# Orders of a slot's steps by table, and two groups of casts on ScalarE: bucketed attention and a gated convolution on one core

## Chip, core and metric

The kernel runs on one core of a Trainium2 chip. The metric is the device time of one execution in microseconds (us). Engines are named as in the profile: PE (TensorE matmuls), PEld (its weight loads), DVE (VectorE), ACT (ScalarE), POOL (GpSimd), and SP, whose queue issues nearly all DMAs.

## The reference, cut to what matters

```python
# attention: B, H, S, D = 4, 8, 768, 64; proj is 64 x 6
q_bits = einsum(q, proj) > 0;  k_bits = einsum(k, proj) > 0       # 6 sign bits: a bucket
mask = q_bucket[..., :, None] == k_bucket[..., None, :]
scores = where(mask, q @ k.T / sqrt(D), -1e9)
attn = exp(scores - max);  attn = attn / (sum(attn) + 1e-9)
x = (attn @ v), heads side by side                               # (4, 768, 512)
# then, per batch
gate = sigmoid(causal convolution of x over the sequence, 5 taps, per channel)
out = (gate * (x @ w_val)) @ w_out                               # 512 x 512 each
```

## The kernel before, in words

There are 32 units (batch, head), each with six tiles of 128 queries: 192 tiles. The main loop runs over slots k = 0 to 195, and slot k works on several tiles at once:

- K, `keep_transposed(k-4)`: two ACT copies (L325) move the transposed probabilities out of PSUM into `pt`. After the sixth tile of a unit it queues `attn_v` for that unit.
- M, F, H, `maxima`, `factors`, `shifts` of tile k: the row maximum and two small DVE steps (L276, L282, L286). R and I, `row_sums` and `recip`, are the DVE's reciprocals for a pair of tiles (L298, L302), in even slots.
- Z, `normalise(k-2)`: POOL multiplies the probabilities by the reciprocals (L307).
- S, `scores(k+1)`: four matmuls (L270) into one of the **two** score buffers `s`. It can start only when the exponential of tile k-1 has read that buffer.
- E, `exponentials(k)`: ACT's exponential with its row sum (L292).
- T, `transposes(k-3)`: six PE transposes (L316) into the two PSUM buffers `tp`, freed by the next slot's K.
- A, one step of `attn_v`: two matmuls (L339; four in the trace, which counts the two parts of each); six steps make a unit, and the last one adds two ACT copies `x` (L347).
- C, one step of `pair_x`, after each second head: first two casts `xh` to fp32r (L359) with their remainders `xl` on POOL (L360), then five convolution steps on DVE (L368, L370), and after the fourth pair of a batch the sigmoids.
- G, one step of `moe`: four matmuls of `x @ w_val` (L401) or of the product with `w_out` (L425). After a value row block the DVE writes the gated values `ht` (L406); in the next G they are cast to `hh` (L410) and POOL makes the remainder `hl` (L412).
- P, one step of `prep` for the next unit: POOL's cast `aq` (L191), POOL's remainder `bq` (L194), six DMAs on SP (L195 to L198, L208, L209), and once in four units the sign bits: twice four matmuls (L226; eight in the trace) into a `tp` buffer and a DVE step `u` (L229).
- W, one step of the weights' decoding: eight parts of 512 columns with five DVE steps, one DVE cast (L113) and two POOL steps (L115, L118) each.

Every slot has the order K M R F I Z H S E C W G P A A T, with A A in odd slots alone, C in odd slots alone up to k = 59, and 1, 0, 2, 0, 2, 2 steps W by k mod 6. PE, ACT, DVE and POOL take their instructions in exactly the order in which this loop writes them; each engine works its own queue in order. SP's order is left to the framework. In the texts below a *head* is the six slots of one unit; the *early stage* is the slots up to 59, with no G yet; the *filled stage* is slots 60 to 191. About a quarter of the filled stage's slots have no G left, since a batch's steps run out before the next batch's sigmoids.

Of the kernel before, what the change touches and what calls it, by code (L numbers as in the profile page):

```python
# [20 lines left out]
TINY = float(2.0 ** -126)  # L21

LEAST = float(2.0 ** -15)


@with_exitstack
def kernel(
# [57 lines left out]
    wo = [const.tile([P, NP, 512], FP32R, name=f"wo{i}") for i in range(2)]  # L85

    def magnitudes(w, t):
        nc.scalar.activation(out=t, in_=w[:, :, 1].bitcast(FP32), func=AF.Abs)  # L90
        return t
# [17 lines left out]
    def split_weight(w, m, hi, lo, ahead):  # L109
        if w.dtype == I32:  # L110
            a, d = yield from from_float64(w, m, ps_m.tile([P, 512], FP32, name="m"))
            yield
            nc.vector.tensor_copy(out=hi, in_=a)  # L113
            yield
            nc.gpsimd.tensor_tensor(out=a, in0=a, in1=hi.bitcast(FP32), op=ALU.subtract)  # L115
            ahead()
            yield
            nc.gpsimd.tensor_tensor(out=lo, in0=a, in1=d, op=ALU.add)  # L118
        else:
            nc.vector.tensor_copy(out=hi, in_=w)  # L120
            ahead()
            yield
            nc.gpsimd.tensor_tensor(out=lo, in0=w, in1=hi.bitcast(FP32), op=ALU.subtract)
# [149 lines left out]
    def maxima(k):  # L273
        s = ss[k]
        nm = small.tile([P, 1], FP32, name="nm")
        nc.vector.tensor_reduce(out=nm, in_=s[:, :, 0:HS], axis=AX.XY, op=ALU.max, negate=True)  # L276
        nms[k] = nm

    def factors(k):

        gs[k] = small.tile([P, 1], FP32, name="gs")
        nc.vector.tensor_scalar(out=gs[k], in0=nms[k], scalar1=BIG / 2, scalar2=scale, op0=ALU.is_lt, op1=ALU.mult)  # L282
# [36 lines left out]
    def keep_transposed(k):  # L319
        i, qt = tiles[k]  # L320
        if qt % 3 == 0:
            cur["pts"].append([ptp.tile([P, 3, HS], FP32, name="pt") for _ in range(2)])
        qo = (qt % 3) * P
        for pt, tp in zip(cur["pts"][-1], tps.pop(k)):
            nc.scalar.copy(out=pt[:, :, qo:qo + P], in_=tp[:, 0:HS].rearrange("p (a b) -> p a b", b=P))  # L325
        if qt == KB - 1:
            avs.append(attn_v(i, cur["pts"]))
            cur["pts"] = []
# [24 lines left out]
    def pair_x(b, c, x, gs, xs_):  # L353
        for o in (0, HS):
            xh = xs.tile([P, HS], FP32R, name="xh")
            xl = xs.tile([P, HS], FP32R, name="xl")
            xs_[(c, o)] = (xh, xl)
            x0 = x[:, KW - 1 + o:KW - 1 + o + HS]
            nc.vector.tensor_copy(out=xh, in_=x0)  # L359
            nc.gpsimd.tensor_tensor(out=xl, in0=x0, in1=xh.bitcast(FP32), op=ALU.subtract)  # L360
        yield
        g = gp.tile([P, S], FP32, name="g")
        gs.append(g)
        for k in range(KW):
            yield
            w = cw_sb[:, c * KW + k:c * KW + k + 1]
            if k == 0:
                nc.vector.tensor_scalar(out=g, in0=x[:, 0:S], scalar1=w, scalar2=None, op0=ALU.mult)  # L368
            else:
                nc.vector.scalar_tensor_tensor(out=g, in0=x[:, k:k + S], scalar=w, in1=g, op0=ALU.mult, op1=ALU.add)  # L370
        if c == NP - 1:
            yield
# [13 lines left out]
    def moe(b, xs_, g):  # L386
        hs = {}
        todo = []

        def later():  # L390
            while todo:
                todo.pop(0)()

        def val(o, j):
            acc = acc_tile()
            m = 0
            for wi, xi in ((0, 0), (1, 0), (0, 1)):
                if m:
                    yield
                for c in range(NP):  # L400
                    nc.tensor.matmul(out=acc[:, 0:HS], lhsT=wv[wi][:, c, j * P:(j + 1) * P],  # L401
                                     rhs=xs_[(c, o)][xi], start=(m == 0), stop=(m == 11))
                    m += 1
                later()
            ht = hp.tile([P, HS], FP32, name="ht", bufs=2)
            nc.vector.tensor_tensor(out=ht, in0=acc[:, 0:HS], in1=g[j][:, o:o + HS], op=ALU.mult)  # L406

            def split():
                hh = hp.tile([P, HS], FP32R, name="hh")
                nc.vector.tensor_copy(out=hh, in_=ht)  # L410
                hl = hp.tile([P, HS], FP32R, name="hl")
                nc.gpsimd.tensor_tensor(out=hl, in0=ht, in1=hh.bitcast(FP32), op=ALU.subtract)  # L412
                hs[(o, j)] = (hh, hl)
            todo.append(split)
            yield

        def outp(o, tb):
            finish(weights)
            acc = acc_tile()
            m = 0  # L420
            for hi, wi in ((0, 0), (0, 1), (1, 0)):
                if m:
                    yield
                for j in range(NP):
                    nc.tensor.matmul(out=acc, lhsT=hs[(o, j)][hi][:, tb * P:(tb + 1) * P],  # L425
                                     rhs=wo[wi][:, j, :], start=(m == 0), stop=(m == 11))
                    m += 1
                later()
            ob = op.tile([P, 512], FP32, name="o")
            if cur["gates"]:  # L430
                nc.vector.tensor_copy(out=ob, in_=acc)
            else:
                nc.scalar.copy(out=ob, in_=acc)
            r0 = o + tb * P
            nc.sync.dma_start(out=out[b, r0:r0 + P, :], in_=ob)
            yield

        def idle(n):
            for _ in range(n):
                later()  # L440
                yield

        def hold():
            while len(moes) < 2 and not cur["end"]:
                yield
# [31 lines left out]
    with tc.manual_schedule(engines=ENGINES):  # L477
        for i in range(5):
            load_raw(i)
        load_values(0)  # L480
        first_prep()
        weights = [load_conv(), load_weights()]
        first_signs()
        preps = [prep(1)]
        step(preps)
        scores(0)
        load_raw(5)
        for gen in weights:
            next(gen)
        for k in range(N + LAG + 1):  # L490
            if 0 <= k - LAG - 1:
                keep_transposed(k - LAG - 1)
            pair = k % 2 == 0 and 0 <= k - 2 < N
            if k < N:
                maxima(k)
            if pair:
                row_sums(k - 2)
            if k < N:
                factors(k)
            if pair:  # L500
                recip(k - 2)
            if 0 <= k - 2 < N:
                normalise(k - 2)
            if k < N:
                shifts(k)
            if k + 1 < N:
                if tiles[k + 1][0] != tiles[k][0]:
                    finish(preps)
                    preps = [prep(tiles[k + 1][0] + 1)]
                scores(k + 1)  # L510
            if k < N:
                exponentials(k)
            if k >= 60 or k % 2:
                step(convs)
            for _ in range((1, 0, 2, 0, 2, 2)[k % 6] if k >= 8 else 0):
                step(weights)
            for _ in range(3 if cur["gates"] else 1):
                step(moes)
            cur["gates"] = max(0, cur["gates"] - 1)
            step(preps)  # L520
            if k % 2:
                step(avs)
                step(avs)
            if 0 <= k - LAG < N:
                transposes(k - LAG)
# [67 lines left out]
```

## Time and profile before

| what | us |
|---|---|
| median of 3 runs | 624.64 (624.13 to 624.96) |
| the profiled execution's own time | 624.6 |
| its span (first to last instruction) | 622.8 |
| slot 0's maximum starts | 10.7 |
| the last tile's maximum starts | 562.1 |

The profile's page gives busy time of each engine over the span. The table of stretches gives the same for a stretch of time. A timeline row has start, duration, engine, line, operation, tiles, count of merged instructions, and, in brackets, how long the engine was idle before it and whose end released it. The span lies 1.8 us under the execution's time, before and after the first and last instruction.

### The profile page before, as it was taken

What the parts mean: (1) busy time and instruction counts of PE and PEld (TensorE: products, weight loads), DVE (VectorE), ACT (ScalarE), POOL (GpSimd) and SP (SyncE); (2) the same over time, 40 slices, a digit from 0 to 9 for tenths busy, and PEclk for the clock granted to TensorE, in tenths of its full rate; (3) what the DMA queues carried; (4) which work ended last, traced back from release to release, by engine and by line L of the source; (5) the groups of instructions that cost most, each with busy time, mean ns of one, the idle gap of its engine ahead of it and who ended that gap; (6) DMA issues with size and microseconds to landing.
All of it is one profiled execution on the core that took longest, in us unless ns stands there. A gap on an engine that the chain in (4) does not pass through costs nothing.

```text
span 622.8 us, 10649 instructions
## 1 busy us (share of the span) xinstructions
PE 587.7 (94%) x3496; PEld 422.6 (68%) x3496; DVE 437.3 (70%) x1032; ACT 420.6 (68%) x881; POOL 376.3 (60%) x362
## 2 busy tenths in 40 slices
PE   5889889889999999999999999999999999999997
PEld 2755555556667777776667776677667777775885
DVE  5687999998757756686757867478675877565632
ACT  3787887777787676577786766677787766765300
POOL 4656878677747665486646766458654776453221
PEclk9799999999999999999999999999999999999999
DMA  8533437333422344233324333233422224100111
GB/s 270 144 99 88 125 109 198 95 102 91 130 51 82 80 123 115 48 88 99 107 80 114 82 98 84 86 82 82 122 55 77 68 47 107 46 19 1 51 52 51
DMA packets 23270, 56.77 MB, mean 91 GB/s; under 512 B 4296, under 2 KB 4296, under 8 KB 23216
## 3 DMA queue, kind: packets, MB, share of 16 engines
q1 hardware_dynamic: 23072, 56.06, 33.4%
q8 instruction: 28, 0.46, 0.3%
q14 instruction: 26, 0.21, 0.1%
q10 hardware_dynamic: 144, 0.03, 0.0%
HBM read 23.12 MB, written 6.29 MB: 47 GB/s over the span
## 4 chain that ended last, share of the span: by engine, by line
PE 69%; ACT 16%; DVE 9%; issue 2%; DMA 1%; POOL 1%; SPq 0%; ACTq 0%; DVEq 0%; POOLq 0%
PE av L339 19%; PE s L270 16%; PE tp L316 13%; PE m L425 8%; ACT p L292 7%; PE m L401 7%; ACT pt L325 5%; DVE nm L276 3%; ACT x L347 3%; PE tp L226 2%; PE tp L425 1%; PE s L425 1%; PE s L401 1%; PE tp L401 1%; DVE g L370 1%
## 5 line engine op out<-in xcount | busy, mean ns | idle before, releaser
L307 POOL TENSOR_SCALAR p<-p,ri 128x768 f32<-128x768 f32 x192 | 208.4, 1090 | 166.1 <-DVE nb L286 142.4
L276 DVE TENSOR_REDUCE nm<-s 128x1 f32<-128x768 f32 x192 | 182.5, 951 | 63.3 <-PE s L270 63.0
L325 ACT COPY pt<-tp 128x384 f32<-128x384 f32 x384 | 166.4, 485 | 87.9 <-PE tp L316 86.8
L292 ACT ACTIVATE p<-s,nb,gs 128x768 f32<-128x768 f32 x192 | 192.6, 1003 | 37.6 <-DVE nb L286 36.4
L316 PEld LDWEIGHTS tp<-ident,p 128*128 128x128 f32 x1152 | 129.8, 141 | 75.9 <-issue 48.1
L316 PE MATMUL tp<-ident,p 128*128 128x128 f32 x1152 | 165.9, 280 | 5.9 <-DVE u L229 2.3
L339 PE MATMUL av<-pt,vt 128*64 128x384 f32 x768 | 144.9, 499 | 0.0
L270 PE MATMUL s<-ak,aq 76*128 76x384 f32 x384 | 116.6, 385 | 20.0 <-ACT p L292 19.2
L270 PE MATMUL s<-bk,bq 128*128 128x384 f32 x384 | 100.0, 341 | 0.0
L339 PEld LDWEIGHTS av<-pt,vt 128*64 128x64 f32 x768 | 47.0, 136 | 62.7 <-issue 62.0
L270 PEld LDWEIGHTS s<-ak,aq 76*128 76x128 f32 x384 | 58.5, 192 | 33.6 <-ACT p L292 32.6
L370 DVE SCALAR_TENSOR_TENSOR g<-x,cw_sb,g 128x768 f32<-128x768 f32 x64 | 78.4, 1226 | 0.2
L270 PEld LDWEIGHTS s<-bk,bq 128*128 128x128 f32 x384 | 70.6, 191 | 0.0
L412 POOL TENSOR_TENSOR hl<-ht,hh 128x384 fp32r<-128x384 f32 x32 | 32.2, 1005 | 47.9 <-DVE hh L410 47.9
L194 POOL TENSOR_TENSOR bq<-r,aq 128x768 fp32r<-128x768 f32 x31 | 57.0, 1840 | 0.1
L347 ACT COPY x<-av 64x384 f32<-64x384 f32 x64 | 30.3, 473 | 31.9 <-PE av L339 31.4
L401 PE MATMUL m<-xh,wv 128*128 128x384 f32 x200 | 43.0, 339 | 0.0
L286 DVE TENSOR_SCALAR nb<-nm,gs 128x1 f32<-128x1 f32 x192 | 39.9, 208 | 3.5
L360 POOL TENSOR_TENSOR xl<-x,xh 128x384 fp32r<-128x384 f32 x32 | 33.4, 1060 | 14.2 <-DVE xh L359 14.2
L406 DVE TENSOR_TENSOR ht<-m,g 128x384 f32<-128x384 f32 x25 | 13.9, 555 | 37.5 <-PE m L401 32.9
L292 ACT ACTIVATION_READ_ACCUMULATOR p<-s,nb,gs 128x1 f32 x192 | 39.2, 204 | 0.0
L425 PE MATMUL m<-wo,hh 128*128 128x512 f32 x144 | 38.4, 396 | 0.0
(88 smaller groups left out, 475.0 us busy)
## 6 DMA issues: line engine op xcount, KB each, us to landing
r<-in_qk_dram SPq DMA_DIRECT2D x32, 384.0 KB
vt<-in_v_dram SPq DMA_DIRECT2D x16, 384.0 KB
out_dram<-o SPq DMA_DIRECT2D x24, 256.0 KB
ak<-aq SPq DMA_DIRECT2D x31, 192.0 KB
bk<-aq SPq DMA_DIRECT2D x31, 192.0 KB
bk<-bq SPq DMA_DIRECT2D x31, 192.0 KB
bq<-aq SPq DMA_DIRECT2D x31, 192.0 KB
w<-in_w_val_dram SPq DMA_DIRECT2D x4, 512.0 KB
```

Of the source, the lines that this page charges most:

```text
L194: nc.gpsimd.tensor_tensor(out=bq, in0=r, in1=aq.bitcast(FP32), op=ALU.subtract)
L270: nc.tensor.matmul(out=s[:, hf, 0:HS], lhsT=lq[0:n, qs], rhs=rk[0:n, hf * HS:(hf + 1) * HS], start=n == M, stop=n == P)
L276: nc.vector.tensor_reduce(out=nm, in_=s[:, :, 0:HS], axis=AX.XY, op=ALU.max, negate=True)
L292: nc.scalar.activation(out=p, in_=s[:, :, 0:HS], func=AF.Exp, bias=nb, scale=gs.pop(k), accum_out=sm[:, k % 2, 0:1])
L307: nc.gpsimd.tensor_scalar(out=p, in0=p, scalar1=rcs.pop(k), scalar2=1.0, op0=ALU.mult, op1=ALU.mult)
L316: nc.tensor.transpose(out=tp[:, n * P:(n + 1) * P], in_=p[:, kb * P:(kb + 1) * P], identity=ident)
L325: nc.scalar.copy(out=pt[:, :, qo:qo + P], in_=tp[:, 0:HS].rearrange("p (a b) -> p a b", b=P))
L339: nc.tensor.matmul(out=av[s * D:(s + 1) * D, 0:HS], lhsT=vt[:, kb, hh * D:(hh + 1) * D], rhs=pt[kb // 3][:, kb % 3, :], start=(kb == 0), s ...
L347: nc.scalar.copy(out=x[hh * D:(hh + 1) * D, o:o + HS], in_=av[s * D:(s + 1) * D, 0:HS])
L370: nc.vector.scalar_tensor_tensor(out=g, in0=x[:, k:k + S], scalar=w, in1=g, op0=ALU.mult, op1=ALU.add)
L401: nc.tensor.matmul(out=acc[:, 0:HS], lhsT=wv[wi][:, c, j * P:(j + 1) * P], rhs=xs_[(c, o)][xi], start=(m == 0), stop=(m == 11))
L425: nc.tensor.matmul(out=acc, lhsT=hs[(o, j)][hi][:, tb * P:(tb + 1) * P], rhs=wo[wi][:, j, :], start=(m == 0), stop=(m == 11))
```

## The change

Three things are changed. (1) The order of a slot's steps comes from a table: six strings for k < 60, by k mod 6, and twelve for k from 60 on, by k mod 12. A letter stands for one step as listed above. (2) The casts `xh` and `hh` are ACT copies; they were DVE copies. (3) In the weights' decoding, the fetched next part's magnitudes (an ACT step, `ahead`) come after the part's last POOL step and not before it; W runs from k = 7 on, six steps per six slots, and from k = 60 on 25 per twelve.

```diff
+START = 60
+EARLY = ["MKRFIHWCCWZPSECT", "MRSKFGGGIHZECPT", "MKGARSFIZHWECPT",
...
+LATE = ["MKRSFIHWZEGWWPCT", "MRKFSWWIHPZPCGWEAPAWT", "MKRSFHIZEGCGWWWT",
...
             nc.gpsimd.tensor_tensor(out=a, in0=a, in1=hi.bitcast(FP32), op=ALU.subtract)
+            yield
+            nc.gpsimd.tensor_tensor(out=lo, in0=a, in1=d, op=ALU.add)
             ahead()
-            yield
-            nc.gpsimd.tensor_tensor(out=lo, in0=a, in1=d, op=ALU.add)
...
-            nc.vector.tensor_copy(out=xh, in_=x0)
+            nc.scalar.copy(out=xh, in_=x0)
...
-                nc.vector.tensor_copy(out=hh, in_=ht)
+                nc.scalar.copy(out=hh, in_=ht)
...
-        for gen in weights:
-            next(gen)
+        next(weights[0])
+        next(weights[1])
         for k in range(N + LAG + 1):
...
+            o = EARLY[k % 6] if k < START else LATE[k % 12]
+            for act in o:
+                if act == "K" and 0 <= k - LAG - 1:
+                    keep_transposed(k - LAG - 1)
...
+                elif act == "C" and (k >= 60 or k % 2):
+                    step(convs)
+                elif act == "W" and k >= 7:
+                    step(weights)
...
+                elif act == "A":
+                    step(avs)
```

The new code has 11 more lines above the loop, so L270 of before is L281 of the changed kernel, L292 is L303, L316 is L327, and so on.

Per twelve slots the counts of S, E, T, K, A, G and of the useful C and P are as before; A comes as 1, 2 and 3 steps in slots 2, 3 and 5 of an early head (2, 2, 2 in slots 3, 5 and 1 before).

**POOL in the early stage.** The rows show one head between the remainders `xl` of a pair (L360, then L371) and the next `MEMSET`; p is Z, w the two weight steps, aq and bq the two preparing steps of the next unit. Before:

```order
L360 TENSOR_TENSOR xl<-x,xh 128x384 x2
L307 TENSOR_SCALAR p<-p,ri 128x768 x2
L191 CAST aq<-r 128x768
L307 TENSOR_SCALAR p<-p,ri 128x768
L115 TENSOR_TENSOR w_726<-w_726,wv_126 128x512
L194 TENSOR_TENSOR bq<-r,aq 128x768
L307 TENSOR_SCALAR p<-p,ri 128x768
L343 MEMSET x 128x4
```

And after:

```order
L371 TENSOR_TENSOR xl<-x,xh 128x384 x2
L318 TENSOR_SCALAR p<-p,ri 128x768 x2
L126 TENSOR_TENSOR w_535<-w_535,wv_126 128x512
L128 TENSOR_TENSOR wv_127<-w_535 128x512
L318 TENSOR_SCALAR p<-p,ri 128x768
L202 CAST aq<-r 128x768
L318 TENSOR_SCALAR p<-p,ri 128x768
L205 TENSOR_TENSOR bq<-r,aq 128x768
L354 MEMSET x 128x4
```

The weight steps moved ahead of aq, and aq and bq moved one slot (one Z) later; no weight step stands between them any more. Before, the weight steps fell at another place in each head.

**PE where the sign bits are made.** The rows show two slots of the filled stage (s is S, m is G, av is A, tp<-ident the transposes, tp<-r the sign bits). Before:

```order
L270 MATMUL s<-bk,bq 128x384 x2
L401 MATMUL m<-xh,wv_127 128x384 x4
L226 MATMUL tp<-r,proj_sb 32x384 x4
L316 MATMUL tp<-ident,p 128x128 x6
L270 MATMUL s<-ak,aq 128x384 x2
L270 MATMUL s<-bk,bq 128x384 x2
L401 MATMUL m<-xl,wv_126 128x384 x4
L226 MATMUL tp<-r,proj_sb 32x384 x4
L339 MATMUL av<-pt,vt 64x384 x4
L316 MATMUL tp<-ident,p 128x128 x6
```

And after:

```order
L281 MATMUL s<-bk,bq 128x384 x2
L237 MATMUL tp<-r,proj_sb 32x384 x8
L412 MATMUL m<-xh,wv_126 128x384 x4
L350 MATMUL av<-pt,vt 64x384 x4
L327 MATMUL tp<-ident,p 128x128 x6
```

Both halves stand in one slot, ahead of G and A; before, one half stood right ahead of the transposes of an even slot.

**ACT after a pair is complete.** The rows show three slots of the filled stage (x is the pair's second head, pt is K, p is E). Before:

```order
L292 ACTIVATE p,sm_119<-s,nb,gs 128x768
L347 COPY x<-av 64x384 x2
L325 COPY pt<-tp 128x3x128 x2
L292 ACTIVATE p,sm_120<-s,nb,gs 128x768
L325 COPY pt<-tp 128x3x128 x2
L292 ACTIVATE p,sm_120<-s,nb,gs 128x768
```

And after:

```order
L303 ACTIVATE p,sm_119<-s,nb,gs 128x768
L358 COPY x<-av 64x384 x2
L336 COPY pt<-tp 128x3x128 x2
L303 ACTIVATE p,sm_120<-s,nb,gs 128x768
L370 CAST xh<-x 128x384 x2
L336 COPY pt<-tp 128x3x128 x2
L421 CAST hh<-ht 128x384
L303 ACTIVATE p,sm_120<-s,nb,gs 128x768
```

Two casts came between an E and the next K, and one between a K and its E.

More of the change, by code (lines that the diff above doesn't have):

```diff
@@ L23 @@
 LEAST = float(2.0 ** -15)
+START = 60
+EARLY = ["MKRFIHWCCWZPSECT", "MRSKFGGGIHZECPT", "MKGARSFIZHWECPT",
+         "MRKSFPPAIHZACEPT", "MKSCRFCICHZCEWT", "MRKISFZHAECWAAWT"]
+LATE = ["MKRSFIHWZEGWWPCT", "MRKFSWWIHPZPCGWEAPAWT", "MKRSFHIZEGCGWWWT",
+         "MSRKFIZHEGAATC", "MSKFRIHECZPCGCT", "MRKFISHZEWPPCGPPAAT",
+         "MKRWCCFCSCIHEWGWZT", "MRWKSFHIZEACAGWPT", "MKRWISFWHEPGZWCT",
+         "MRKFISHCGZEAAWT", "MKFPRSIHEWZWWGT", "MRSKPIFHWZEAAPWT"]
 @with_exitstack
@@ L115, in split_weight @@
             nc.gpsimd.tensor_tensor(out=a, in0=a, in1=hi.bitcast(FP32), op=ALU.subtract)
-            ahead()
             yield
             nc.gpsimd.tensor_tensor(out=lo, in0=a, in1=d, op=ALU.add)
+            ahead()
         else:
@@ L487 @@
         load_raw(5)
-        for gen in weights:
-            next(gen)
+        next(weights[0])
+        next(weights[1])
         for k in range(N + LAG + 1):
[L491 to L525, printed above, removed]
@@ new lines @@
+            o = EARLY[k % 6] if k < START else LATE[k % 12]
+            for act in o:
+                if act == "K" and 0 <= k - LAG - 1:
+                    keep_transposed(k - LAG - 1)
+                elif act == "M" and k < N:
+                    maxima(k)
+                elif act == "R" and k % 2 == 0 and 0 <= k - 2 < N:
+                    row_sums(k - 2)
+                elif act == "F" and k < N:
+                    factors(k)
+                elif act == "I" and k % 2 == 0 and 0 <= k - 2 < N:
+                    recip(k - 2)
+                elif act == "Z" and 0 <= k - 2 < N:
+                    normalise(k - 2)
+                elif act == "H" and k < N:
+                    shifts(k)
+                elif act == "S" and k + 1 < N:
+                    if tiles[k + 1][0] != tiles[k][0]:
+                        finish(preps)
+                        preps = [prep(tiles[k + 1][0] + 1)]
+                    scores(k + 1)
+                elif act == "E" and k < N:
+                    exponentials(k)
+                elif act == "C" and (k >= 60 or k % 2):
+                    step(convs)
+                elif act == "W" and k >= 7:
+                    step(weights)
+                elif act == "G":
+                    for _ in range(3 if cur["gates"] else 1):
+                        step(moes)
+                    cur["gates"] = max(0, cur["gates"] - 1)
+                elif act == "P":
+                    step(preps)
+                elif act == "A":
+                    step(avs)
+                elif act == "T" and 0 <= k - LAG < N:
+                    transposes(k - LAG)
```

## The prediction

> **What bounds the kernel now.** First the page's busy times, then the table of stretches for the early stage, the last early head, the filled stage and the end (columns: length, then busy us of PE, PEld, DVE, ACT, POOL).
>
> ```profile
> PE 587.7 (94%) x3496; PEld 422.6 (68%) x3496; DVE 437.3 (70%) x1032; ACT 420.6 (68%) x881; POOL 376.3 (60%) x362
> 52.05:147.93 95.88, 85.11 (x521) 55.57 (x521) 87.71 (x205) 75.17 (x163) 75.53 (x73) 1.00 0.46 125
> 147.93:162.92 14.99, 13.93 (x84) 9.21 (x84) 12.51 (x30) 11.73 (x27) 10.85 (x11) 1.00 0.43 112
> 162.92:562.00 399.08, 392.23 (x2384) 286.36 (x2384) 274.28 (x665) 287.61 (x602) 246.15 (x230) 1.00 0.32 82
> 562.00:623.00 61.00, 55.63 (x283) 44.49 (x280) 26.77 (x43) 12.74 (x23) 15.57 (x15) 1.00 0.10 39
> ```
>
> There are two regimes. From 52 to 148 us, DVE is busy 87.71 of 95.88 us (91%), and six heads take 95.88/6 = 15.98 us each. The next head, in which the weights are decoded and only convolution steps are left, takes 14.99 at 12.51 us of DVE. From 163 us on PE is busy 98% and the granted clock is 1.00: only small holes are left. The work of PE is the same before and after, so the change can gain what the holes hold, and no more.
>
> Next the waits, and a stretch without G, to see which hole returns.
>
> ```profile
> PEld s L270 <- ACT p L292: 32.6, 52, 2.3
> 302.80 0.87 PE L316 MATMUL tp<-ident,p 128*128 128x128 f32 x6
> 303.38 0.86 ACT L325 COPY pt<-tp 128x384 f32<-128x384 f32 x2 [1.25 <-PE tp L316]
> 303.43 0.59 PE L270 MATMUL s<-ak,aq 76*128 76x384 f32 x2
> 304.12 1.01 ACT L292 ACTIVATE p<-s,nb,gs 128x768 f32<-128x768 f32 x1
> 304.21 0.82 PE L316 MATMUL tp<-ident,p 128*128 128x128 f32 x6
> 305.28 0.62 PE L270 MATMUL s<-ak,aq 76*128 76x384 f32 x2 [0.25 <-ACT p L292]
> ```
>
> S waits for E, which frees the score buffer. In a slot with neither A nor G, PE needs 0.78 us for S (303.43 to 304.21) and 0.63 for T (302.80 to 303.43), 1.41 in all. But K waits for the transposes just done, E stands behind K on ACT, and the next S behind E: 303.43 to 305.28, **1.85 us, is the floor of any slot**, since K still stands ahead of E in every string of the new tables. An early head has three such slots before and after. That is why the head without decoding already stands at 14.99, and I take 15.0 as the floor of an early head.
>
> **The early stage: DVE's queue.** One chain, read from the cast to the stall:
>
> ```profile
> 129.33 0.62 DVE L359 CAST xh<-x 128x384 fp32r<-128x384 f32 x2
> 129.77 2.01 POOL L360 TENSOR_TENSOR xl<-x,xh 128x384 fp32r<-128x384 f32 x2 [2.85 <-DVE xh L359]
> 129.87 0.95 DVE L276 TENSOR_REDUCE nm<-s 128x1 f32<-128x768 f32 x1
> 131.04 0.21 DVE L286 TENSOR_SCALAR nb<-nm,gs 128x1 f32<-128x1 f32 x1
> 131.35 0.99 ACT L292 ACTIVATE p<-s,nb,gs 128x768 f32<-128x768 f32 x1 [0.74 <-DVE nb L286]
> 132.49 0.62 PE L270 MATMUL s<-ak,aq 76*128 76x384 f32 x2 [1.09 <-ACT p L292]
> ```
>
> The casts stand right ahead of M (129.87); M, F, H and E follow, and S waits for E. Gone from DVE, they let this chain start up to 0.54 us earlier (129.33 to 129.87).
>
> How much DVE work leaves a head? The stretch 52 to 148 has six casts, 2.27 us:
>
> ```profile
> 52.05:147.93 95.88, 2.27 (x6) 1.00 0.46 125
> L98 DVE TENSOR_SCALAR m<-m 128x512 int32<-128x512 int32 x8 | 5.6, 699 | 0.3
> L101 DVE SCALAR_TENSOR_TENSOR w<-w,m 128x512 int32<-128x512 int32 x8 | 5.5, 684 | 0.3
> L113 DVE CAST wo<-w 128x512 fp32r<-128x512 f32 x4 | 2.1, 532 | 0.0
> ```
>
> (The first row is of L359 alone.) That is 2.27/6 = 0.38 us a head. Decoding a part takes five steps of 0.68 to 0.70 and one of 0.53, 4.0 us; a part has six steps W, so a head did 7/6 of a part, 4.65 us, and now does one, 4.0. Together 1.0 us of 14.62 (87.71/6) leaves, and 13.6 is left against a floor of 15.0: the same 91% as now if the head falls to the floor, so some waits stay. I take 15.4 a head, between 15.0 and 15.98. Six heads: 6 x 0.58 = 3.5 us. The seven-sixths return at the end, because decoding now reaches slot 59 and the head at 147.93 is no longer free of it: 15.4 for 14.99, +0.4. The sign bits, twice in this stage, stand ahead of A A in one slot now; I give them 0.4. **Early stage: -3.5** (from 0 to -6.3, all heads at the floor).
>
> **The next unit's operands.** aq and bq stand one slot later on POOL. What lies behind them is SP's queue:
>
> ```profile
> 85.89 1.30 POOL L115 TENSOR_TENSOR w<-w,wv 128x512 f32<-128x512 f32 x1 [2.81 <-DVE wv L113]
> 90.52 1.82 POOL L194 TENSOR_TENSOR bq<-r,aq 128x768 fp32r<-128x768 f32 x1
> 92.36 0.46 SPq L197 DMA_DIRECT2D bk<-bq  x1
> 95.05 0.50 SPq L198 DMA_DIRECT2D bq<-aq  x1
> 98.86 0.61 PE L270 MATMUL s<-ak,aq 76*128 76x384 f32 x2 [0.39 <-ACT p L292]
> ```
>
> L197 follows bq at once; L198 needs its landing, 2.7 us later, and if its own landing takes as long (an estimate from the same row), the operands are there at 97.8, 1.1 us before the S that reads them. So the slack is thin. It is thin here because POOL stood 2.81 us at a weight step whose cast was late; in the new order the weight steps come two slots behind their cast and none stands between aq and bq. One saves up to 2.8 us, the other costs a slot of 1.85 or more: I cost the sum at nothing, with +6 as the upper end (see the rivals).
>
> **The filled stage.** Three holes:
>
> ```profile
> 245.88 0.87 PE L316 MATMUL tp<-ident,p 128*128 128x128 f32 x6
> 246.51 0.59 PE L270 MATMUL s<-ak,aq 76*128 76x384 f32 x2
> 248.88 0.55 PE L316 MATMUL tp<-ident,p 128*128 128x128 f32 x3
> 249.82 0.55 PE L316 MATMUL tp<-ident,p 128*128 128x128 f32 x3 [0.40 <-DVE u L229]
> 250.13 0.60 PE L270 MATMUL s<-ak,aq 76*128 76x384 f32 x2
> 155.72 0.59 PE L270 MATMUL s<-ak,aq 76*128 76x384 f32 x2
> 156.82 0.85 PE L316 MATMUL tp<-ident,p 128*128 128x128 f32 x6
> 158.09 0.62 PE L270 MATMUL s<-ak,aq 76*128 76x384 f32 x2 [0.43 <-ACT p L292]
> ```
>
> *Sign bits.* Transposes to next S take 0.63 us (245.88 to 246.51), but 1.25 (248.88 to 250.13) where they need the buffer that u has still to clear. With both halves ahead of G and A, the 1.4 us and more of A hide u. Five such places: -3.0. *The copies x.* The slot after them takes 2.37 us (155.72 to 158.09) for 1.85: ACT's two copies wait for the last A and push K and E. In a slot with G of 0.7 us, 0.3 of it is left open. A now stands ahead of G for second heads, and a second G fills the slot after first heads; of some 22 places I count half: -2.0 (0 to -6). *The 1.85 floor in slots without G* stays.
>
> **What the casts cost on ACT.**
>
> ```profile
> L359 DVE CAST xh<-x x32: 341/380/1189, 62.7 to 576.8; 128x384 fp32r<-128x384 f32 x32
> L410 DVE CAST hh<-ht x32: 348/354/1164, 184.9 to 610.5; 128x384 fp32r<-128x384 f32 x32
> L325 ACT COPY pt<-tp x384: 452/485/522, 19.3 to 571.5; 128x384 f32<-128x384 f32 x192
> L433 ACT COPY o<-m x12: 585/587/597, 223.9 to 578.8; 128x512 f32<-128x512 f32 x12
> L251 ACT CAST aq<-r 64x768 fp32r<-64x768 f32 x1 | 0.8, 832 | 1.6 <-DMA r<-in_qk_dram 1.6
> ```
>
> (Source rows: min/median/max ns.) No ACT cast of this shape is in the trace. By the copies, 485 ns for 384 columns and 587 for 512, 0.8 ns a column; the cast of 768 columns at 832 is some 40 more than that line gives, so 0.52 us (bounds 0.45, the least copy, and 0.83). 64 casts are 33 us of ACT, of which 48 casts, 25 us, fall in the filled stage, where ACT has 399 - 288 = 111 us free. A cast behind E in a slot without A delays the next K, but that next slot has A A and is about 1 us longer than ACT's work; ahead of E it shows only where ACT is late. I count +1.5 (0 to +25).
>
> The maxima of both casts show a second effect: 1.16 to 1.19 us where the median is 0.35 to 0.38, three times as long with the same data. The Trainium skill ("SBUF — State Buffer", Who interferes with whom) says that DVE and POOL hold a shared port pair exclusively, and that copies and casts on DVE can take it while ScalarE has ports of its own; by it all 64 casts shed this loss, and the sum stays, since the 0.38 us a head was measured with the loss in it. The trace agrees in the three-fold maxima. Against the change stands "VectorE: DVE Perf Modes" of the Trainium skill, the perf-mode tier table: an fp32 copy between SBUF tiles runs at two elements a cycle there. The rows agree, 0.35 us against ACT's estimated 0.52; by it alone, with nothing hidden, the sum would be 64 x 0.17 = 10.9 us worse, 628.4.
>
> **The end.** PE waits little after 562 (55.63 of 61.00 busy, the rest the last result's way out). DVE no longer casts behind `ht`: -0.7 (0 to -1.3).
>
> **Sum.** Against the profiled execution's 624.6, equal to the median of 624.64: -3.5 early, -3.0 and -2.0 and +1.5 filled, -0.7 end, together -7.7, so 616.9; with a little of the unseen handovers, 617.5.
>
> **Rivals.**
>
> *ACT becomes the late engine (slower).* An even slot of the filled stage with G has 2.1 to 2.3 us of PE against ACT's 1.85; a cast makes it 2.37. If 32 of the 48 casts there show 0.3 us each, that is +9.6 in place of +1.5: 617.5 + 8.1 = 625.6; if half of all 64 show in full (32 x 0.52 = 16.6), 632. It decides where S waits for E more than 1.5 us more per batch than now. For it: K and E are already S's releaser in 52 waits. Against: the odd slots' slack. Middle 628. The tier table of the Trainium skill points this way.
>
> *The operands come late (slower).* If aq and bq end a slot later in all eight early heads and the decoding step's wait is not what held them, each S at a head's start waits 0.8 to 1.9 us: 8 x 1.4 = 11, so about 628.5.
>
> *Nothing moves.* If K-E-S, not DVE's queue, already sets early heads, -3.5 goes; if x and cast costs cancel, only the sign bits are left against new holes: 624.
>
> *More goes.* All heads at 15.0 (-6.3), the x holes closed (-6), -3, -1.3, casts hidden: about 610 to 613.
>
> **Chances.** Forecast (614.5 to 622) 0.50, more 0.14, nothing 0.14, ACT 0.12, operands 0.10. Faster and slower mean by over 0.2% (1.25 us, about what a measurement of this kernel can tell). Faster 0.64, same 0.14, slower 0.22. The range leaves out the lower end of "more" and the upper half of the two slower cases: 611.5 to 627.5.
>
> **What would show it.** Early heads (S to S over six slots) of 15.4, not 16 or 17; DVE's share there unchanged while its busy time falls by about 1 us a head; no wait of T for u; the ACT casts at 0.5 us. It is wrong if S at a head's start waits for a DMA, if ACT's casts take 0.8, or if S's waits for E grow after 163 us.

## The result, and the profile after

The changed kernel takes 614.59 us (median of 4 runs, 614.31 to 615.73); the kernel before took 624.80 in the runs beside it. The ratio is 0.984, 95% interval 0.9825 to 0.9859: 10 us faster. The forecast was 617.5 us with a range of 611.5 to 627.5. The profiled span went from 622.8 to 612.3 us.

First the answers of the changed kernel to the rows shown in the prediction: busy times of the engines from the page, the two waits that the holes were read from (us in total, times, longest), and the two casts on ScalarE (min/median/max ns).

```profile
PE 582.7 (95%) x3496; PEld 425.2 (69%) x3496; DVE 407.9 (67%) x968; ACT 444.8 (73%) x945; POOL 365.3 (60%) x362
PEld s L281 <- ACT p L303: 31.4, 47, 2.3
PE tp L327 <- DVE u L240: 0.3, 1, 0.3
L370 ACT CAST xh<-x x32: 508/527/542, 60.8 to 566.6; 128x384 fp32r<-128x384 f32 x32
L421 ACT CAST hh<-ht x32: 496/516/549, 181.4 to 599.9; 128x384 fp32r<-128x384 f32 x32
```

ScalarE carries 24 us more, and the wait of S for E has not grown (52 waits of 32.6 us before, 47 of 31.4 now). The wait of the transposes for u, which the prediction counted at five places, is there once.

Where the 10.5 us of the two spans lie is read from the table of stretches. A head runs from its first S to the first S of the next; the stretches are heads 2 to 9, heads 10 to 30, and the rest. The columns are start and end, length, then the busy us (and instructions) of PE, PEld, DVE, ACT and POOL, the granted clock, the DMA share and GB/s. First the kernel before, then the changed one:

```profile
34.84:162.92 128.08, 114.52 (x704) 74.30 (x704) 114.35 (x268) 100.00 (x217) 96.26 (x93) 1.00 0.44 116
162.92:544.49 381.57, 374.78 (x2277) 272.87 (x2277) 263.80 (x638) 275.44 (x575) 237.16 (x221) 1.00 0.33 85
544.49:622.80 78.31, 73.08 (x391) 57.98 (x389) 37.25 (x70) 24.90 (x50) 24.55 (x24) 1.00 0.09 34
```

```profile
33.67:157.77 124.10, 113.48 (x704) 75.97 (x705) 112.82 (x263) 102.38 (x225) 94.32 (x91) 1.00 0.44 120
157.77:534.25 376.48, 371.08 (x2272) 273.22 (x2273) 241.98 (x597) 289.84 (x616) 228.03 (x223) 1.00 0.33 86
534.25:612.30 78.05, 73.60 (x395) 58.76 (x393) 31.04 (x55) 32.25 (x65) 24.34 (x24) 0.99 0.09 34
```

The early heads gave 4.0 us (128.08 to 124.10), the filled heads 5.1 (381.57 to 376.48), the end 0.3. The remaining 1.2 us lie ahead of head 2, where executions of one program differ by as much. TensorE's granted clock dips at the start, and the moment at which it comes back differs: from 21 to 24 us it was 0.74 in the kernel before and 1.00 in the changed one. `e_early_only` (below), which has the same program up to slot 59 as the changed kernel, had 0.61 there and reached head 2 at 35.20 us, where the changed kernel did at 33.67. So heads are compared below by their own lengths, and whole kernels by their medians.

The early heads also show that the prediction had the right queue and the wrong reason. Rows of the timeline around the first two slots of head 7, before:

```profile
115.89 0.62 PE L270 MATMUL s<-ak,aq 76*128 76x384 f32 x2 [0.24 <-ACT p L292]
...
116.35 1.25 DVE L370 SCALAR_TENSOR_TENSOR g<-x,cw_sb,g 128x768 f32<-128x768 f32 x1
...
117.52 0.68 DVE L97 TENSOR_SCALAR m<-o 128x512 f32<-128x512 f32 x1
...
118.23 0.70 DVE L98 TENSOR_SCALAR m<-m 128x512 int32<-128x512 int32 x1
118.84 0.94 DVE L276 TENSOR_REDUCE nm<-s 128x1 f32<-128x768 f32 x1
118.86 0.60 PE L270 MATMUL s<-ak,aq 76*128 76x384 f32 x2
...
120.33 0.99 ACT L292 ACTIVATE p<-s,nb,gs 128x768 f32<-128x768 f32 x1 [0.65 <-DVE nb L286]
...
121.46 0.44 PE L270 MATMUL s<-ak,aq 76*128 76x384 f32 x1 [1.00 <-ACT p L292]
```

Scores have two buffers, so the S two slots on waits for this slot's E, and E for this slot's M. M begins 2.95 us after its S (115.89 to 118.84), behind a convolution step and a weight step. From M to E pass 1.49 us, from E to the S that waits for it 1.13. So slots 0 and 1 last 2.95 + 1.49 + 1.13 = 5.57 us together, and since slot 0 takes 2.97 (118.86 less 115.89), slot 1 takes 2.60 in place of its floor of 1.85. The same sum, M's lateness less 0.35 but not under 1.85, against slot 1 as measured before:

```
head                   3     4     5     7     8     9
M after S, slot 0    2.80  2.96  2.34  2.95  2.66  1.99
slot 1, by the sum   2.45  2.61  1.99  2.60  2.31  1.85
slot 1, measured     2.45  2.61  1.99  2.60  2.30  1.85
```

The sum is a least value. Of the two heads with sign bits, head 2 fits as well (M 3.01 behind, slot 1 is 2.66 by the sum and as measured), and head 6 does not (M 1.67 behind, 1.85 by the sum, 2.29 measured). There M was not the late step: on ACT a weight step (L90, from 101.70 us) stood ahead of K, which began only at 102.27.

In the changed kernel the same M comes 1.00 to 1.49 us behind its S (here 112.13 to 113.62), a convolution step ahead of it as before, but no weight step:

```profile
112.13 0.62 PE L281 MATMUL s<-ak,aq 76*128 76x384 f32 x2 [0.61 <-ACT p L303]
...
113.62 0.94 DVE L287 TENSOR_REDUCE nm<-s 128x1 f32<-128x768 f32 x1
...
115.75 0.60 PE L281 MATMUL s<-ak,aq 76*128 76x384 f32 x2
...
117.61 0.44 PE L281 MATMUL s<-ak,aq 76*128 76x384 f32 x1 [0.24 <-ACT p L303]
```

Slot 0 now holds three steps A in place of two and takes 3.62 us (3.74 in head 2), slot 1 takes 1.85 in every early head from head 2 on (1.85 to 1.86), and slot 2, which lost the A, takes 2.34 in place of 2.97. Over heads 2 to 9, slot 0 grew by 5.3 us and slot 2 shrank by 5.0, while slot 1 went from 18.77 to 14.83: slot 1 alone makes 3.9 of the 4.0 us.

Two things changed together here, and no run parts them: M comes earlier, and slot 0 is longer by an A. By the sum either would nearly do alone. With M as late as before (2.95 us) but slot 0 at 3.62, slot 1 would take 1.95; with M at 1.49 and slot 0 at 2.97 it would take its floor of 1.85.

### The profile page after: what moved, and what is told of

Its sections match the earlier page's. It is cut to its first block, busy times and chain, and to the rows that moved or that the text cites. A ratio compares the mean times of both kernels' runs of the same rounds, so it can differ in the third digit from the quotient of the medians.

```text
span 612.3 us, 10635 instructions
## 1 busy us (share of the span) xinstructions
PE 582.7 (95%) x3496; PEld 425.2 (69%) x3496; DVE 407.9 (67%) x968; ACT 444.8 (73%) x945; POOL 365.3 (60%) x362
## 4 chain that ended last, share of the span: by engine, by line
PE 75%; ACT 13%; DVE 7%; POOL 2%; issue 2%; DMA 1%; SPq 0%; POOLq 0%; ACTq 0%; DVEq 0%
PE av L350 19%; PE s L281 17%; PE tp L327 14%; PE m L412 9%; PE m L436 8%; ACT p L303 7%; ACT pt L336 4%; DVE nm L287 3%; PE tp L237 1%; PE tp L412 1%; PE tp L436 1%; PE s L436 1%; ACT x L358 1%; PE s L412 1%; POOL p L318 1%
## 5 line engine op out<-in xcount | busy, mean ns | idle before, releaser
L318 POOL TENSOR_SCALAR p<-p,ri 128x768 f32<-128x768 f32 x192 | 191.6, 1008 | 133.9 <-DVE nb L297 50.4
L303 ACT ACTIVATE p<-s,nb,gs 128x768 f32<-128x768 f32 x192 | 192.8, 1004 | 28.1 <-DVE nb L297 26.6
L327 PEld LDWEIGHTS tp<-ident,p 128*128 128x128 f32 x1152 | 132.1, 141 | 53.5 <-issue 36.6
L327 PE MATMUL tp<-ident,p 128*128 128x128 f32 x1152 | 162.5, 277 | 0.9 <-DVE u L240 0.3
L281 PE MATMUL s<-ak,aq 76*128 76x384 f32 x384 | 116.7, 385 | 19.4 <-ACT p L303 19.2
L281 PE MATMUL s<-bk,bq 128*128 128x384 f32 x384 | 100.5, 343 | 0.0
L281 PEld LDWEIGHTS s<-ak,aq 76*128 76x128 f32 x384 | 58.4, 192 | 36.4 <-ACT p L303 31.4
L281 PEld LDWEIGHTS s<-bk,bq 128*128 128x128 f32 x384 | 70.8, 191 | 0.2 <-DMA bq<-aq 0.2
L381 DVE SCALAR_TENSOR_TENSOR g<-x,cw_sb,g 128x768 f32<-128x768 f32 x64 | 70.1, 1095 | 0.2
L423 POOL TENSOR_TENSOR hl<-ht,hh 128x384 fp32r<-128x384 f32 x32 | 33.6, 1051 | 61.2 <-ACT hh L421 57.4
L205 POOL TENSOR_TENSOR bq<-r,aq 128x768 fp32r<-128x768 f32 x31 | 58.8, 1898 | 1.0
L371 POOL TENSOR_TENSOR xl<-x,xh 128x384 fp32r<-128x384 f32 x32 | 33.4, 1065 | 34.9 <-ACT xh L370 34.9
L303 ACT ACTIVATION_READ_ACCUMULATOR p<-s,nb,gs 128x1 f32 x192 | 39.4, 205 | 0.0
L412 PEld LDWEIGHTS m<-xh,wv 128*128 128x128 f32 x200 | 35.0, 188 | 6.3 <-issue 6.0
```

Source lines behind the costliest of these rows:

```text
L205: nc.gpsimd.tensor_tensor(out=bq, in0=r, in1=aq.bitcast(FP32), op=ALU.subtract)
L281: nc.tensor.matmul(out=s[:, hf, 0:HS], lhsT=lq[0:n, qs], rhs=rk[0:n, hf * HS:(hf + 1) * HS], start=n == M, stop=n == P)
L303: nc.scalar.activation(out=p, in_=s[:, :, 0:HS], func=AF.Exp, bias=nb, scale=gs.pop(k), accum_out=sm[:, k % 2, 0:1])
L318: nc.gpsimd.tensor_scalar(out=p, in0=p, scalar1=rcs.pop(k), scalar2=1.0, op0=ALU.mult, op1=ALU.mult)
L327: nc.tensor.transpose(out=tp[:, n * P:(n + 1) * P], in_=p[:, kb * P:(kb + 1) * P], identity=ident)
```

## The experiments

Every time below is a median beside runs of the kernel before on the same chip; in the three groups that stood at 624.65, 624.53 and 624.34 us. The ratio to it has its 95% interval.

```
run                 us      ratio to before
e_order_only      616.24   0.9878 [0.9853, 0.9903]
e_casts_only      624.89   1.0012 [0.9998, 1.0026]
e_early_only      622.59   0.9969 [0.9955, 0.9982]
e_late_only       627.18   1.0059 [1.0035, 1.0082]
e_late_old_ahead  619.33   0.9926 [0.9908, 0.9944]
e_ahead_old       614.53   0.9842 [0.9825, 0.9858]
e_early_w         620.88   0.9937 [0.9919, 0.9956]
e_w_place         637.53   1.0224 [1.0200, 1.0249]
e_x_old           620.94   0.9945 [0.9931, 0.9959]
e_bits_old        622.85   0.9971 [0.9959, 0.9982]
e_half_only       615.40   0.9855 [0.9837, 0.9873]
e_opnd_old        617.69   0.9895 [0.9878, 0.9911]
```

### The orders alone, and the casts alone

`e_order_only` puts both casts of the changed kernel back on VectorE:

```diff
-            nc.scalar.copy(out=xh, in_=x0)
+            nc.vector.tensor_copy(out=xh, in_=x0)
...
-                nc.scalar.copy(out=hh, in_=ht)
+                nc.vector.tensor_copy(out=hh, in_=ht)
```

> The changed kernel with both groups of casts back on DVE; the orders stay. By the prediction's terms the casts are worth -2.3 us in the early stage (6 heads x 0.38), -0.7 at the end and +1.5 in the filled stage, -1.5 together: so about 616, with early heads of 15.3 to 15.6 in place of 14.9 to 15.2. Rival (the casts carry the gain, because they also end DVE's stalls against POOL): 619 or more. Rival (the casts only cost ACT): 614 or less.

`e_casts_only` is the kernel before with the opposite edit of these two lines, and nothing else.

> The kernel before with both groups of casts on ACT; its order stays. By the prediction's terms 624.7 - 1.5 = about 623, with early heads of 15.6 to 15.8. Rival (the casts carry the gain): 620 or less. Rival (ACT becomes late where the order was not made for it): over 626.

The orders carry 8.4 of the 10 us; the casts alone do nothing that can be measured (+0.2 us, interval -0.1 to +1.6), where 1.5 us of gain were expected. The 1.6 us that the casts add to the new orders are at the edge of what the two intervals set apart. In stretches of the same heads, first with the orders alone, then with the casts alone:

```profile
33.63:158.61 124.98, 113.36 (x705) 76.03 (x705) 115.30 (x271) 99.44 (x217) 92.52 (x90) 1.00 0.43 119
158.61:535.50 376.89, 370.42 (x2272) 272.48 (x2273) 256.58 (x638) 275.36 (x575) 232.82 (x224) 1.00 0.33 86
```

```profile
35.51:163.66 128.15, 115.21 (x705) 74.15 (x705) 113.15 (x260) 102.99 (x225) 95.88 (x92) 1.00 0.42 116
163.66:545.76 382.10, 375.31 (x2277) 273.25 (x2277) 247.83 (x597) 290.75 (x616) 236.05 (x222) 1.00 0.32 85
```

With the old order the early heads take 128.15 us though DVE is rid of the eight casts that they hold; with the new one 124.98 though it has them and is busy for longer than before (115.30 us against 114.35). On ACT the casts cost 0.5 us of the filled heads alone (382.10 against 381.57), and with the new orders they gain 0.4 there and 0.9 in the early heads (124.98 to 124.10).

### One table at a time

`e_early_only` keeps the changed kernel up to slot 59 and goes on in the old order:

```diff
-LATE = ["MKRSFIHWZEGWWPCT", "MRKFSWWIHPZPCGWEAPAWT", "MKRSFHIZEGCGWWWT",
...
+LATE = ["KMRFIZHSECWWGPT", "KMRFIZHSECWWGPAAT"] * 6
```

> The changed kernel with the old order from slot 60 on. By the two traces the first 60 slots gained 5.2 us and the rest 5.1: so about 619.5, and 620 to 621 if the casts need the new order of the filled stage to be hidden (the prediction counted +1.5 for them). Rival (most of the gain is in the filled stage's order): 622 or more.

`e_late_only` does the reverse: the old order up to slot 59 and the new table behind it, casts and weight start as in the changed kernel.

```diff
-EARLY = ["MKRFIHWCCWZPSECT", "MRSKFGGGIHZECPT", "MKGARSFIZHWECPT",
-         "MRKSFPPAIHZACEPT", "MKSCRFCICHZCEWT", "MRKISFZHAECWAAWT"]
+EARLY = ["KMRFIZHSECWGPT", "KMRFIZHSECGPAAT", "KMRFIZHSECWWGPT",
+         "KMRFIZHSECGPAAT", "KMRFIZHSECWWGPT", "KMRFIZHSECWWGPAAT"]
```

> The changed kernel with the old order up to slot 59. About 619.5 by the same split, less what the casts alone bring to the early stage (2.3 by the prediction): 617 to 619.5, early heads of 15.6 to 15.8 against 14.9 to 15.2. Rival (the early order brings nothing, the casts all of the early gain): 615.

The first gained 2 us, where some 4 to 5 were expected; its heads 2 to 9 take 124.2, as in the changed kernel, and it then loses 1.7 us in heads 10 and 11 (17.60 and 21.47 us against 16.34 and 21.06 before), where the old order takes over. So the 622 us that its rival names were reached for another reason than the rival's. The second was slower than before, which no theory had named. Its filled heads do keep the gain (376.9 us), but its heads 3 to 5 take 19.63, 17.69 and 16.29 us in place of 15.59, 15.74 and 15.48. Its timeline there shows DVE held by ScalarE:

```profile
51.48 0.67 ACT L101 ACTIVATE o<-w 128x512 f32<-128x512 f32 x1
...
52.18 0.70 DVE L108 TENSOR_SCALAR m<-o 128x512 f32<-128x512 f32 x1 [2.33 <-ACT o L101]
...
55.00 0.99 ACT L303 ACTIVATE p<-s,nb,gs 128x768 f32<-128x768 f32 x1 [2.10 <-DVE nb L297]
...
56.13 0.62 PE L281 MATMUL s<-ak,aq 76*128 76x384 f32 x2 [1.26 <-ACT p L303]
```

The magnitudes of a weight part (L101) start one weight step later in the change. Where the old order has two W in one slot, that puts L101 and L108, which reads it, one behind the other, and M, E and S queue behind L108. Two runs test this. `e_late_old_ahead` is `e_late_only` with the start at its old place:

```diff
             nc.gpsimd.tensor_tensor(out=a, in0=a, in1=hi.bitcast(FP32), op=ALU.subtract)
+            ahead()
             yield
             nc.gpsimd.tensor_tensor(out=lo, in0=a, in1=d, op=ALU.add)
-            ahead()
```

> The old order up to slot 59, the new one from slot 60, the casts on ScalarE, and the next weight part started where the kernel before started it (behind POOL's subtraction, one step earlier). Theory: the run with the old early order lost some 7 us in the heads 3 to 5 because the moved start put the magnitudes of a part (ACT L101) and the first DVE step that reads them one right behind the other; with the old start those heads take 15.5 to 16 us again, the filled stage keeps its -5, and the time is 619 to 620.5. Rival: the two stages are coupled in another way (the old early order hands over a worse state), or the loss lies in the casts on ScalarE under the old order: heads 3 to 5 stay above 16.5 us and the time at 624 or more.

It came out as the theory had it: heads 3 to 5 take 15.62, 15.77 and 15.33, and the time is 619.33. One moved line was worth 7.9 us under the old early order. `e_ahead_old` makes the same edit in the changed kernel:

> The changed kernel with only the start of the next weight part back at its old place (ScalarE's magnitudes one weight step earlier). Theory of the prediction: with the new order it is worth nothing either way, since no DVE step of the next part follows in the same slot: 614 to 615.2. Rival: the later start is a part of the early gain, by as much as it cost under the old order (7.9 us), or a good part of it: 616 or more.

There it is worth nothing, 614.53 for 614.59.

### What the early heads gain by

`e_early_w` takes one W from the old early order and leaves the rest of `e_late_old_ahead` as it is, so that a head decodes one weight part, as in the changed kernel:

```diff
-         "KMRFIZHSECGPAAT", "KMRFIZHSECWWGPT", "KMRFIZHSECWWGPAAT"]
+         "KMRFIZHSECGPAAT", "KMRFIZHSECWWGPT", "KMRFIZHSECWGPAAT"]
```

> As the run beside it with the old early order and the old start, but one W less in the last slot of each early head, so that a head decodes one weight part in place of 7/6. Theory of the prediction (DVE's load sets the early head: the seventh W is 0.65 of the 1.03 us of DVE work that leaves): the early heads fall by some 0.4 us each, heads 2 to 9 together by 2.5 to 3.5, and the time is 2 to 3 us below the run beside it, about 617. Rival: what counts is the place of the steps within a slot, not their number: heads 2 to 9 fall by less than 1 us and the time stays within 1 us of the run beside it.

The load is not it: heads 2 to 9 take 127.7 us together against 128.1, and 620.88 us can't be told from 619.33 by their intervals. Single heads swing between 14.97 (head 8) and 16.70 (head 9). The sum above still gives slot 1 of each: in head 9 M starts 3.26 us behind S, which makes slot 1 2.91; it took 2.92. The rest of that swing lies mostly in slot 5 (1.85 against 2.50), where the sum gives 1.85 and 2.18.

`e_w_place` keeps six W a head in the new order and moves one of them by two slots:

```diff
-EARLY = ["MKRFIHWCCWZPSECT", "MRSKFGGGIHZECPT", "MKGARSFIZHWECPT",
+EARLY = ["MKRFIHWCCWWZPSECT", "MRSKFGGGIHZECPT", "MKGARSFIZHECPT",
```

> The changed kernel with one weight step W of each early head moved from the third slot to the first, so that three W stand between the maxima of slots 0 and 1; still six W a head. Theory: not DVE's load but its place decides: the maxima of slot 1 come 0.5 to 0.7 us later behind S in the heads where the third step is DVE's, the short slot 1 (1.85 us) becomes 2.3 to 2.6 there, and heads 2 to 9 lose 1.5 to 4 us: 616 to 618.5. Rival (the load of a head decides): heads 2 to 9 within 0.6 us of 124.1 and the time within 1 us of 614.6.

It lost 23 us, several times what was expected: heads 2 to 9 take 145.5 us. Head 5 of it, from S of slot 1 on:

```profile
95.45 0.59 PE L281 MATMUL s<-ak,aq 76*128 76x384 f32 x2
...
96.15 0.70 ACT L101 ACTIVATE o<-w 128x512 f32<-128x512 f32 x1
...
96.89 0.69 DVE L108 TENSOR_SCALAR m<-o 128x512 f32<-128x512 f32 x1 [1.94 <-ACT o L101]
...
99.01 0.95 DVE L287 TENSOR_REDUCE nm<-s 128x1 f32<-128x768 f32 x1
...
101.63 0.62 PE L281 MATMUL s<-ak,aq 76*128 76x384 f32 x2 [1.32 <-ACT p L303]
```

M of slot 1 starts at 99.01, 3.56 us behind its S; 3.56 + 1.49 + 1.13 = 6.18 us for slots 1 and 2, and S follows at 101.63, 6.18 later. But the run isn't a clean test of a step's place: the third W is again an L108 right behind its L101, and that wait, 15.8 us in eight parts by the view of waits, is most of the 21 us that the early heads lost. What both runs show is that the number of W does not set the head, and that a late M costs what the sum says. They do not test the moved A.

### The filled heads

`e_x_old` undoes three strings of the late table, those of the two copies x (A) and of the G beside them:

```diff
-         "MRWKSFHIZEACAGWPT"
+         "MRWKSFHIZECGWPAAT"
...
-         "MRSKPIFHWZEAAPWT"
+         "MRSKPIFHWZEGAAPWT"
...
-         "MKRSFHIZEGCGWWWT"
+         "MKRSFHIZEGCWWWT"
```

> The changed kernel with the two A behind G again in the eighth late string, G back in the twelfth and only one G in the third, as the order before had them; nothing else moved. Theory of the prediction: the slots behind the copies x get their 0.3 us holes back at about half of 22 places, and with the rest of the filled gain (5.1 less 3.6 for the sign bits) the time is 1 to 2 us above the changed kernel, 615.6 to 616.6. Rival: these places gave nothing, and the remaining 1.5 us come from the casts that left DVE: within 0.6 us of 614.6.

It lost 6.3 us, where 1 to 2 were expected. Of the 22 heads from head 10 on, 13 lose 0.27 to 0.49 us, 4.2 together, heads 16 and 24 lose 0.9 each, and the other seven 0.12 or less. Two stretches from S to S in heads 20 and 21 show it. First `e_x_old`, with G ahead of A in slot 0 and one G in slot 3:

```profile
339.27 0.59 PE L277 MATMUL s<-ak,aq 76*128 76x384 f32 x2
...
340.06 0.87 PE L408 MATMUL m<-xl,wv 128*128 128x384 f32 x4
340.86 1.51 PE L346 MATMUL av<-pt,vt 128*64 128x384 f32 x8
...
342.93 0.59 PE L277 MATMUL s<-ak,aq 76*128 76x384 f32 x2
...
348.65 0.60 PE L277 MATMUL s<-ak,aq 76*128 76x384 f32 x2
...
351.02 0.62 PE L277 MATMUL s<-ak,aq 76*128 76x384 f32 x2
```

Then the changed kernel, with two G in the second stretch:

```profile
336.46 0.59 PE L281 MATMUL s<-ak,aq 76*128 76x384 f32 x2
...
339.40 0.59 PE L281 MATMUL s<-ak,aq 76*128 76x384 f32 x2
...
345.13 0.59 PE L281 MATMUL s<-ak,aq 76*128 76x384 f32 x2
...
345.92 0.87 PE L412 MATMUL m<-xh,wv 128*128 128x384 f32 x4
346.63 0.86 PE L412 MATMUL m<-xl,wv 128*128 128x384 f32 x4
347.33 0.82 PE L327 MATMUL tp<-ident,p 128*128 128x128 f32 x6
347.91 0.59 PE L281 MATMUL s<-ak,aq 76*128 76x384 f32 x2
```

A G costs 0.72 us where A fills the slot (3.66 against 2.94) and 0.41 where the copies x had left a hole (2.78 against 2.37): 0.3 us gained. A ahead of G in the odd head gives nearly as much (3.70 + 2.07 for 3.65 + 2.38). The whole pair of heads went from 35.44 us before to 34.87, and back to 35.53 in `e_x_old`.

`e_bits_old` puts the P of the late table back to one behind G in each slot. The text on record speaks of the sign bits; the edit also moved POOL's operand steps, which are P too.

```diff
-"MRKFSWWIHPZPCGWEAPAWT", "MKRSFHIZEGCGWWWT"
+"MRKFSWWIHZCGPWEAAWT", "MKRSFHIZEGCGPWWWT"
...
-"MRKFISHZEWPPCGPPAAT", "MKRWCCFCSCIHEWGWZT"
+"MRKFISHZEWCGPAAT", "MKRWCCFCSCIHEWGPWZT"
```

> The changed kernel with the two P of the sign bits apart again and behind G in the late strings, as before; nothing else moved. Theory: the stall of the second transposes behind DVE's u (0.6 us at each of five heads) comes back, and with it 3 to 3.6 us: 617.6 to 618.2, and a wait of the transposes for u shows in the trace. Rival: the sign-bit heads are shorter because of the steps around them (A, W, C), and the time stays within 1 us of 614.6.

It lost 8.3 us, spread over heads with and without sign bits. Two runs part it, from slot 66 on: `e_half_only` moves the two halves alone and leaves POOL's order as it is, `e_opnd_old` moves aq and bq alone and leaves TensorE's.

```diff
+LATER = {1: "MRKFSWWIHZCGWEAAWT", 2: "MKRSFHIZEGPCGWWWT", 3: "MSRKFIZHEGPAATC"}
```

> The changed kernel with only the two halves of the sign bits moved from slot k%12 = 1, ahead of G and A, to one half behind G in each of the next two slots, from slot 66 on; POOL's order is the changed kernel's, the early stage too. It divides the run before, which had moved these halves and POOL's operand steps together and lost 8 us. Theory of the prediction: heads 14, 18, 22 and 26 lose 0.6 to 0.9 us each, 2.5 to 3.5 together: 617 to 618, with a wait of the transposes for u in the trace. Rival: the operand steps on POOL were the whole loss: within 1 us of 614.6.

```diff
+LATER = {0: "MKRSFIHWZEGPWWCT", 1: "MRKFSWWIHPPZPCGWEAAWT", 5: "MRKFISHZEWCGPAAT",
+         6: "MKRWCCFCSCIHEWGPWZT", 11: "MRSKIFHWZEPAAWT"}
```

> The changed kernel with only POOL's operand steps (aq and bq) at their old places from slot 66 on: aq behind G in the slot after S of the new unit, bq a slot later; TensorE's order is the changed kernel's. The prediction costed their move at nothing. Theory after the run before: where bq (1.9 us) stands ahead of a normalise, the transposes wait 0.7 us for POOL (L318); the heads 11, 13, 15 and so on lose 0.3 to 0.9 us each, 3.5 to 5 us together: 618 to 619.5. Rival: POOL's lateness is hidden as predicted, and the loss came from the halves alone: within 1 us of 614.6.

The halves cost 0.8 us, which the intervals do not set apart from nothing. The transposes wait for u again, three times in place of once:

```profile
PE tp L327 <- DVE u L240: 1.1, 3, 0.4
```

But the two waits that are new stand in heads 18 and 26, which do not grow: in head 18 the three slots concerned take 2.97 + 3.04 + 3.74 = 9.75 us with the halves apart and 4.39 + 2.37 + 2.98 = 9.74 together. Heads 14 and 22 do grow (19.71 for 19.02, 20.37 for 20.14), without that wait. The edit leaves a second G between the half and the transposes there:

```profile
242.65 0.85 PE L237 MATMUL tp<-r,proj_sb 128*32 128x384 f32 x8
243.43 0.97 PE L412 MATMUL m<-xl,wv 128*128 128x384 f32 x4
244.24 0.82 PE L327 MATMUL tp<-ident,p 128*128 128x128 f32 x6
```

So in these two heads this run does not bring the old stall back. `e_bits_old` does: there the half stands right ahead of the transposes, which wait 0.35 us for u, and the slot takes 0.52 us more than here in both heads (4.27 for 3.75, 4.74 for 4.22).

The operands cost 3.1 us, 0.86 of them in each of the heads 15, 21 and 29. In head 21:

```profile
360.50 1.01 POOL L423 TENSOR_TENSOR hl<-ht,hh 128x384 fp32r<-128x384 f32 x1 [4.19 <-ACT hh L421]
...
361.46 1.82 POOL L205 TENSOR_TENSOR bq<-r,aq 128x768 fp32r<-128x768 f32 x1
...
363.25 1.79 POOL L318 TENSOR_SCALAR p<-p,ri 128x768 f32<-128x768 f32 x2
364.22 0.87 PE L327 MATMUL tp<-ident,p 128*128 128x128 f32 x6 [0.65 <-POOL p L318]
```

hl and bq stand in a row ahead of the normalise, and the transposes wait for it. The slot takes 4.57 us here. In the kernel before it took 3.66, with bq at the same place in the string, because POOL got there sooner: hl ran 2.6 us ahead of bq, and bq began 1.2 us before the slot's S (366.36 against 367.55), where here it begins 1.2 behind it. After the change it takes 3.70. So this is not a gain of the change over the kernel before. It is a cost that the other moves of the new table would have made, and that the earlier aq and bq avoid.

The rest of the loss of `e_bits_old` lies in heads 10 and 11 (20.84 + 19.52 us against 18.74 + 18.70), where the two runs, which start at slot 66, show none, and in heads 14 and 22, where the old stall stands.

## Why the prediction was right, and where it wasn't

- **The early heads, -3.5: right in size (-4.0), wrong in its reason.** The step that failed is the working from DVE's load, "Together 1.0 us of 14.62 (87.71/6) leaves". In the six heads of that sum, 3 to 8, DVE's busy time fell from 87.71 to 84.96 us, 0.46 a head in place of 1.0. With the orders alone DVE was busy for longer than before, and the heads still gained 3.1. The casts' 0.38 us a head gave nothing alone (128.15 us), the seventh W 0.4 us in eight heads. What gained is slot 1, by an earlier M, a longer slot 0, or both. The six heads take 15.41 us on average for a forecast of 15.4, and that is luck: the mean holds head 6, whose sign bits left it at 17.05 (17.03 before), while heads 3 to 5 and 7 to 9 stand at 14.89 to 15.23, near the floor.
- **The operands, 0: right.** The weight loads of S wait 0.2 us for them in the whole kernel. The undoing in the late table costs 3.1 us, but only in the new order.
- **The sign bits, -3.0: too large.** The stall was counted in full, 0.6 us at five places. It is worth 0.52 in heads 14 and 22 and nothing in heads 18 and 26, where the slots have no G; head 10 was not tested by itself. That the slots without G have room for it fits the equal sums of head 18. Keeping the halves apart costs these two heads another 0.9 together, which the prediction did not count.
- **The copies x, -2.0: the right hole, too small a size.** "I count half" of 22 places was near, with 13 heads that show it; but each gives some 0.3 us or more, 4.2 together. The term was also added up wrong: half of 22 places at the prediction's own 0.3 is 3.3, not 2.0. The 0.9 us of heads 16 and 24 stand apart: head 16 was no longer before the change (16.35 us for 16.31).
- **The casts on ACT, +1.5: too high.** Their duration was right, 0.52 us (medians 516 and 527 ns), and they are hidden: +0.5 us of the filled heads in the old order, -0.4 in the new one. The sum by the Trainium skill's perf-mode tier table ("VectorE: DVE Perf Modes"), 10.9 us worse with nothing hidden, is not what the runs show (its 628.4 also adds the 10.9 to a sum that already holds +1.5 for the same casts). The prediction's second effect, casts of 1.16 to 1.19 us on DVE, is gone too: on ACT none takes more than 0.55. The casts alone show that this was worth nothing either under the old order.
- **The end, -0.7: it gave 0.3.**
- **The sum.** The filled heads gave 5.1 us for a forecast of 3.5. The 4.2 of the copies and the 0.9 of the halves make as much, but that shows little: undone one by one, the copies, the operands and the halves cost 6.3, 3.1 and 0.8 us, 10.2 together. Head by head it doesn't close either: heads 18 and 19 gave 0.98 us (39.06 to 38.08), of which undoing the copies takes back 0.28, and heads 24 and 25 lost 0.56 (33.32 to 33.88) to the change. G stands in other slots there; what each of these moves is worth wasn't separated.
- **The rivals.** ACT as the late engine fell: S waits for E no longer than before. Late operands and nothing moving fell too. The case that more goes, 610 to 613 us, was nearer on the copies' holes.

No variant that was run beats the changed kernel beyond the spread of its runs.

## What to carry to other kernels

With a buffer that turns in two slots, two neighbouring slots last at least the lateness of the first consumer plus the chain to the buffer's release; work out that sum slot by slot, and place the other steps where it leaves slack, rather than adding up an engine's load. Two steps of one chain on different engines should not stand in the same gap of the order: one moved line that put them there cost 7.9 us under one order and nothing under another. The parts of such a table don't add up when they are undone one by one, so an undone part shows what it is worth in this order, not its share of the gain. And an undone part is only a test of a stall if the trace shows that the stall came back in the place that got slower.

## What the runs showed of the hardware that wasn't expected

The granted clock fell to half in the middle of a kernel without a long pause of TensorE. In `e_late_only`, in stretches of 3 us:

```profile
54.00:57.00 3.00, 1.74 (x13) 1.47 (x12) 2.86 (x7) 1.83 (x4) 0.00 (x0) 1.00 0.71 205
57.00:60.00 3.00, 1.28 (x9) 1.04 (x8) 2.83 (x9) 1.64 (x4) 1.68 (x2) 0.94 0.01 5
60.00:63.00 3.00, 3.00 (x12) 1.29 (x10) 1.40 (x5) 1.18 (x3) 2.48 (x3) 0.50 0.23 52
```

PE was busy 1.74 and 1.28 of 3 us, and in these six us its waits for E were 1.26 and 1.72 us; then the clock stood at 0.50, and A's eight matmuls took 2.53 us where they take 1.51. `e_w_place` shows the same twice (0.50 in 48 to 51 us, 0.58 in 69 to 72). The Trainium skill ("TensorE: Matmul & The Clock Gate", HAM oscillation — how this bites in real kernels) gives as a rule that gaps of TensorE over some 3.4 us throttle it; here a busy share of about half over six us, in shorter gaps, came ahead of the drop. It does not always bring one: in `e_w_place` PE was busy 3.49 of 6 us ahead of the 0.58 (63 to 69 us), and 3.45 of 6 from 99 to 105 us, where the clock stayed at 1.00. What decides between the two isn't shown. So a stall on this engine can cost twice: about 1 us of the loss in head 3 is the slow A behind it.
